# A float32 kernel of linear attention beside an MLP: three small moves of side work

## The chip, the cores and the metric

The kernel runs on one core of a Trainium2 chip. The metric is the time of one execution on the device, in microseconds (us). The kernel before took 713.92 us (median of three executions, 712.97 to 714.16).

## The reference

```python
x  = A_x                                     # 1 x 2048 tokens x 640
xn = layernorm(x)
# A: linear attention, 32 heads of 20, learned feature maps
q, k, v = split_heads(xn @ wqkv)
phi(u) = concat(softmax(u @ w_phi), softmax(-(u @ w_phi)))
o = phi(q) @ (phi(k).T @ v) / (phi(q) @ sum(phi(k)) + 1e-6)
A = merge_heads(o) @ wo
# B: an MLP over a second layernorm, hidden width 1728, tanh gelu
B = gelu(layernorm(xn) @ w1 + b1) @ w2 + b2
return x + A + B
```

## The kernel before, in words

All products are done in float32 split into two parts: a high part (a copy in the short float32r format) and a low part (the value less its high part). A full product takes three matmuls, high x high, high x low and low x high (`mm3`, L62 to L64). So every operand needs a copy on ScalarE and a subtraction on VectorE or GpSimd before TensorE can use it.

The 2048 tokens are four blocks of 512. First the MLP is computed for blocks 0 and 1, then keys, values and queries are projected, then the MLP for blocks 2 and 3 runs with the attention beside it, then the output projection. This text is about the first of these stages, from 50 to 215 us.

The hidden width is cut into 14 chunks of 128, of which chunk 13 is half a chunk (64). Chunks go in pairs, group g being chunks 2g and 2g+1. For a group and a block, the first layer fills one PSUM bank a chunk, ScalarE applies gelu, and a high and a low part are made; the second layer (`second`) then runs for m = 0 to 4 through three PSUM banks in turn: six matmuls (five with the half chunk) into a bank, and then VectorE adds the bank to the accumulator (L313, L311 for group 0). So the bank of m can be filled again for the third m after it only once VectorE has added it up. For groups 2 to 5 a scheme with fewer products is used (`cycle`), whose second layers stand between the products of the next group.

Group 6 holds the half chunk. In `passes` its 64 rows of high weight and its 64 rows of low weight share one matmul, and so L288 to L292 follow: ScalarE copies half of the bank, VectorE adds the other half (L289), ScalarE applies gelu (L290) and makes the high part (L291), and L292 makes the low part, which only the second layer of that block reads. `self.tail` says which engine does L292: in this stage VectorE, in the later MLP stage GpSimd.

Beside the MLP runs a chain of side work, a generator called `side` (`prep`). TensorE's code advances it once after each three matmuls; one such advance is called a step here. `prep` first waits two steps; then VectorE subtracts a column from the feature-map weights (L681, into the tile `wpt`), and at the same step the first *folds* follow (L612: small matmuls of the key and query weights with `wpt`, into two further banks, which ScalarE and VectorE then copy out, L630 and L632). After the folds, ten chunks of x of blocks 2 and 3 are normalised: a load (L674), GpSimd subtracts the mean (L695), VectorE multiplies (L703), ScalarE makes the high part (L709), VectorE the low part (L712), and both are stored (L714). The last of the ten falls in group 6.

In group 6 a second chain, `last_weights`, loads the v weights (L821), makes their high parts on ScalarE and their low parts on GpSimd (L53 and L56 through `split`, tiles `wkh` and `wkl`), and copies the k weights in (L823).

ScalarE, VectorE and GpSimd do their work in the order in which this code issues it, each engine strictly in order; so an instruction that waits holds up all behind it. The loads and stores go through one queue (SP), whose order a scheduler of the framework decides when the program is built.

Of the kernel before, what the change touches and what calls it, by code (L numbers as in the profile page):

```python
# [11 lines left out]
ALU = mybir.AluOpType  # L12
# [26 lines left out]
def f(ap):  # L39
    return ap.bitcast(F32)  # L40
# [3 lines left out]
def tile_kernel(ctx: ExitStack, tc: tile.TileContext, x, xT, wkT, wqT, wv, wphi, wo, w1, b1, w2, b2,  # L44
                ident, mmask, emask, vsel, out):
    nc = tc.nc
    ctx.enter_context(nc.allow_low_precision(reason="float32 operands are split exactly into float32r parts"))

    def split(hi, lo, src, scale=None, eng=nc.vector, first=nc.scalar):

        if scale is None:
            if first is nc.scalar:
                nc.scalar.activation(hi, src, AF.Copy)  # L53
            else:
                first.tensor_copy(hi, src)
            eng.tensor_tensor(lo, src, f(hi), op=ALU.subtract)  # L56
        else:
            nc.scalar.activation(hi, src, AF.Copy, scale=scale)
            nc.vector.scalar_tensor_tensor(lo, src, scale, f(hi), op0=ALU.mult, op1=ALU.subtract)
# [37 lines left out]
    class Banks:  # L97

        def __init__(self, *ids):
            self.ids, self.n = ids, 0  # L100
# [11 lines left out]
    def mtile(i, dtype=F32):  # L112
        return mp.tile([P, 2, D if i < 5 else 512], dtype, name=f"m{i}")
# [87 lines left out]
    class Mlp:  # L201
        def __init__(self, slots, hid):
            self.hid, self.turn, self.slots, self.beside, self.raw, self.tiles, self.spare = hid, 0, slots, iter(()), {}, {}, nc.vector
            self.tail = nc.gpsimd
            self.ph, self.px, self.po = Banks(0, 1, 2), Banks(3, 4), Banks(5, 6, 7)
            self.hold, self.held = False, []

# [59 lines left out]
        def passes(self, g, b, ws, hid=None):  # L267


            yh, yl = y[b]  # L270
            self.turn ^= 1
            todo = ()
            if hid is None:
                hid, todo, gts = [], ws, mtile(4)
            for j, (w1h, w1l, w2h, w2l) in enumerate(todo):
                gt = gts[:, j, :512]
                hs = mtile(self.hid[self.turn][j], F32R)
                hh, hl = hs[:, 0, :512], hs[:, 1, :512]
                if not (g == 6 and j == 1):
                    self.first(g, j, b, ws[j], gt, hh, hl)  # L280
                    hid.append((hh, hl))
                else:
                    pz = self.ph()
                    for kc in range(KC):
                        nc.tensor.matmul(pz, w1h[:, kc, :], yh[:, kc, :], start=kc == 0, stop=False)  # L285
                        nc.tensor.matmul(pz, w1l[:, kc, :], yl[:, kc, :], start=False, stop=kc == KC - 1)  # L286
                    tm = gt[0:64, :]
                    nc.scalar.activation(tm, pz[64:128, :], AF.Copy)  # L288
                    nc.vector.tensor_tensor(tm, pz[0:64, :], tm, op=ALU.add)  # L289
                    nc.scalar.activation(gt[0:64, :], tm, AF.Gelu_apprx_tanh, bias=b1t[0:64, 13:14])  # L290
                    nc.scalar.activation(hh[0:64, :], gt[0:64, :], AF.Copy)  # L291
                    self.tail.tensor_tensor(hh[64:128, :], gt[0:64, :], f(hh[0:64, :]), op=ALU.subtract)  # L292
                    hid.append((hh, None))
            yield
            yield from self.second(g, b, hid, ws)
# [28 lines left out]
    mlp = Mlp((0, 1, 2, 3), ((0, 2), (1, 3)))  # L324

    def finish(p):
        for _ in p:
            pass
# [66 lines left out]
    raw = [mlp.raw[c] for c in range(2)]  # L395
# [106 lines left out]
    def hi(t, src, eng=None):  # L502
        return lambda: nc.scalar.activation(t[0], src, AF.Copy)

    def lo(t, src, eng):
        return lambda: eng.tensor_tensor(t[1], src, f(t[0]), op=ALU.subtract)
# [72 lines left out]
    def raws(n, g):  # L579
        raw = fp.tile([P, D], F32, name="raw")  # L580
        if g < 5:
            nc.sync.dma_start(raw, {"k": wkT, "q": wqT}[n][g * G6:g * G6 + P, :])
        else:
            nc.sync.dma_start(raw[:2 * DH], wkT[5 * G6:])
            nc.sync.dma_start(raw[2 * DH:], wqT[D - P + 2 * DH:])
        return raw
# [64 lines left out]
    def ahead(loads, n):  # L651

        todo, ready = iter(loads), []
        for _ in loads:
            while len(ready) <= n:
                load = next(todo, None)
                if load is None:
                    break
                ready.append(load())
            yield ready.pop(0)  # L660
# [10 lines left out]
    def prep():  # L671
        def load(b, c):
            xc = fp.tile([P, D], F32, name="raw")[:, :512]
            nc.sync.dma_start(xc, xT[c * P:(c + 1) * P, b * 512:(b + 1) * 512])  # L674
            return xc

        todo = [(b, c) for b in range(2, 4) for c in range(KC)]
        loads = ahead([*(lambda job=job: raws(*job) for job in jobs), *(lambda job=job: load(*job) for job in todo)], 1)
        for _ in range(2):
            yield  # L680
        nc.vector.tensor_tensor(wpt[:, :, :, 1:], wpt[:, :, :, 1:], wpt[:, :, :, 0:1].to_broadcast([P, 6, 6, DF]), op=ALU.subtract)  # L681
        more = chain(more_stats(), rows(fp, mlp.px))
        for i, _ in enumerate(folds(loads)):
            if i % 10 in (5, 7, 9):
                next(more, None)
            yield
        fs.close()
        finish(more)
        mrs = [row_pair(b, fp.tile([P, 2, 512], F32, name="t", bufs=2).rearrange("p a c -> p (a c)")) for b in range(2, 4)]
        for _ in range(6):  # L690
            yield

        def centred(b, c):
            xc = next(loads)
            nc.gpsimd.tensor_tensor(xc, xc, mrs[b - 2][:, 0], op=ALU.subtract)  # L695
            return xc

        following = centred(*todo[0])
        for _ in range(4):
            yield  # L700
        for i, (b, c) in enumerate(todo):
            xc = following
            nc.vector.tensor_tensor(xc, xc, mrs[b - 2][:, 1], op=ALU.mult)  # L703
            yield
            if i + 1 < len(todo):
                following = centred(*todo[i + 1])
            yield
            hi = fp.tile([P, D], F32R, name="xs", bufs=3)[:, :512]
            nc.scalar.activation(hi, xc, AF.Copy)  # L709
            for _ in range(2):  # L710
                yield
            nc.vector.tensor_tensor(xc.bitcast(F32R), xc, f(hi), op=ALU.subtract)  # L712
            for p, src in enumerate((f(hi), xc)):
                nc.sync.dma_start(y_dram[b - 2][p][:, c, :], src)  # L714
            for _ in range(4):
                yield
# [9 lines left out]
    def cycle(g, other, side):  # L726
# [3 lines left out]
        bank, v, a = {}, nc.vector, nc.scalar  # L730
# [35 lines left out]
        if g < 5:  # L766
            events += weight_events({"11": 3, "S1": 4, "S3": 5, "s1": 7, "s2": 10, "S4": 11, "D5": 12, "12": 15, "15": 16, "s3": 18,
                                       "22": 22, "25": 23, "s4": 27, "d5": 28}, g + 2)
        else:
            def take(c):  # L770
                def go():
                    mlp.raw[c] = araw[c - 12], r2[c - 12]
                    ready[c] = mlp.take_parts(c, mlp.tiles[c % 4])
                    ready[c][1][0]()
                return go

            mlp.spare, mlp.tail = nc.gpsimd, nc.vector
            events += [(16, take(12)), (19, take(13))]
        mlp.beside = both(at_steps(*((when - 1, what) for when, what in events)), side)
        bank["a"] = mlp.ph()  # L780
# [27 lines left out]
    for g in range(2, 6):  # L808
        before = cycle(g, before, side)
# [3 lines left out]
    wkv_ = [kvw.tile([P, KC, CB[2]], F32R, name=f"wk{p}") for p in "hl"]  # L813

    def last_weights():

        events = []
        for kc in range(KC):
            k, v = slice(0, F1), slice(F1 + 2 * F2, CB[2])
            raw = f(wkv_[1][:, kc, v])  # L820
            events += [(2 * kc, lambda kc=kc, raw=raw: nc.sync.dma_start(raw, wv_dram[:, kc])),  # L821
                       (2 * kc + 7, lambda kc=kc, raw=raw: split(wkv_[0][:, kc, v], wkv_[1][:, kc, v], raw, eng=nc.gpsimd)),
                       *((2 * kc + 10 + p, lambda kc=kc, p=p: nc.sync.dma_start(f(wkv_[p][:, kc, k]), wk_dram[p][:, kc])) for p in range(2))]  # L823
        return at_steps(*events)

# [36 lines left out]
    for i in range(2):  # L862
        v = vp.tile([P, 11 * VS], F32R, name=f"v{i}")
# [121 lines left out]
    for t, i in [(t, i) for t in range(13) for i in range(4)] + [(13, 0), (13, 1), (13, 2), (14, 0), (14, 1), (13, 3), (14, 2), (15, 0), (15, 1),  # L985
# [30 lines left out]
        if i == 0 and t in (1, 2, 3, 6, 7):  # L1016

            kc = (1, 2, 3, 6, 7).index(t)
# [7 lines left out]
        if (t, i) == (11, 0):  # L1026
            mlp = Mlp((0, 2, 3, 1), ((1, 2), (0, 3)))
# [305 lines left out]
    for g in range(7):  # L1333
        for b in range(2, 4):
# [24 lines left out]
            if (g, b) == (0, 3):  # L1359
# [5 lines left out]
                op = ctx.enter_context(tc.tile_pool(name="oB", bufs=1, reuse_waits="tile"))  # L1365
# [189 lines left out]
```

## Time and profile before

| | |
|---|---|
| median of the runs | 713.92 us (712.97 to 714.16) |
| profiled execution, whole | 713.56 us |
| its span, first to last instruction | 711.8 us |
| TensorE busy | 701.5 us, 99% |
| VectorE, GpSimd, ScalarE busy | 507.6, 439.4, 352.9 us |

Times of the trace count from the first instruction. PE is TensorE, DVE VectorE, ACT ScalarE, POOL GpSimd, SP the queue that issues transfers. Matmuls are pipelined: one may start 0.23 us after the one before it although its row shows 0.39 us, so it is the starts that tell the pace.

### The profile page before, as it was taken

Reading aid. Unit: us, or ns where it says so; the run is one execution under the profiler, and the core shown is the slowest. Engines: PE = TensorE matmul, PEld = TensorE weight load, DVE = VectorE, ACT = ScalarE, POOL = GpSimd, SP = SyncE. Lnnn points to the kernel's source line nnn. Section 1 sums busy time; section 2 is a strip of 40 time slices with the busy share of each in tenths; the row PEclk is TensorE's granted clock in tenths of the full one; section 3 lists DMA queues with packets and bytes.
Section 4 is the critical chain, followed back from the end, with each engine's and each line's share of the span. In section 5 each row is a group of like instructions: output and inputs, shape, how many; then the busy total and the mean of one; then the engine's idle time right before and its main releaser. Section 6 shows DMA issues by size and latency. Waiting matters only on the chain.

```text
span 711.8 us, 9916 instructions
## 1 busy us (share of the span) xinstructions
PE 701.5 (99%) x3368; PEld 592.2 (83%) x3368; DVE 507.6 (71%) x839; ACT 352.9 (50%) x624; POOL 439.4 (62%) x408
## 2 busy tenths in 40 slices
PE   8999999999899999999999999999999999999998
PEld 7888888888678888888888888888888888888886
DVE  7877875588554798898878887755575656778653
ACT  7844646445513564464355448455565556551310
POOL 2586434676442897797787878656587777553400
PEclk9999999999999999999999999999999999999999
DMA  9615966557651223723600705674444653163222
GB/s 328 267 41 196 297 176 195 136 183 236 260 231 83 93 75 148 182 93 151 148 1 1 186 0 189 165 212 128 134 129 120 206 157 105 46 234 120 90 75 88
DMA packets 77894, 105.05 MB, mean 148 GB/s; under 512 B 22884, under 2 KB 46068, under 8 KB 76220
## 3 DMA queue, kind: packets, MB, share of 16 engines
q1 hardware_dynamic: 77844, 104.43, 46.6%
q8 instruction: 26, 0.43, 0.3%
q14 instruction: 24, 0.20, 0.1%
HBM read 71.43 MB, written 34.61 MB: 149 GB/s over the span
## 4 chain that ended last, share of the span: by engine, by line
PE 90%; DMA 4%; DVE 2%; ACT 1%; POOL 1%; issue 1%; SPq 1%; ACTq 0%
PE bank L62 27%; PE bank L63 27%; PE bank L64 27%; PE bank L946 3%; DMA r<-in_w 2%; DMA wv__79<-in_wv 2%; PE bank L612 2%; PE bank L1175 1%; PE bank L1174 1%; PE bank L308 1%; PE bank L309 1%; DMA raw<-in_wkT 1%; PE bank L286 0%; PE bank L285 0%; DVE acc L311 0%
## 5 line engine op out<-in xcount | busy, mean ns | idle before, releaser
L62 PE MATMUL bank<-m,w 128*128 128x512 f32 x266 | 105.8, 398 | 4.0 <-DVE acc L313 3.7
L62 PE MATMUL bank<-y,w 128*128 128x512 f32 (+1 forms) x270 | 104.6, 387 | 0.0
L64 PE MATMUL bank<-m,w 128*128 128x512 f32 x266 | 104.3, 392 | 0.0
L64 PE MATMUL bank<-y,w 128*128 128x512 f32 (+1 forms) x270 | 104.3, 386 | 0.0
L63 PE MATMUL bank<-y,w 128*128 128x512 f32 (+1 forms) x270 | 104.2, 386 | 0.0
L63 PE MATMUL bank<-m,w 128*128 128x512 f32 x262 | 102.7, 392 | 0.0
L313 DVE TENSOR_TENSOR acc<-bank,acc 128x512 f32<-128x512 f32 x120 | 80.6, 681 | 23.3 <-PE bank L64 18.9
L62 PE MATMUL bank<-wkh,y 128*128 128x512 f32 (+2 forms) x240 | 87.6, 365 | 0.0
L63 PE MATMUL bank<-wkl,y 128*128 128x512 f32 (+2 forms) x240 | 87.1, 363 | 0.0
L64 PE MATMUL bank<-wkh,y 128*128 128x512 f32 (+2 forms) x240 | 86.9, 362 | 0.0
L911 POOL TENSOR_TENSOR m<-m,mx 128x640 f32<-128x640 f32 (+2 forms) x48 | 44.4, 937 | 47.8 <-DVE mx L899 47.8
L892 ACT ACTIVATE m<-bank 128x512 f32<-128x512 f32 (+1 forms) x64 | 26.5, 440 | 87.2 <-PE bank L64 66.6
L1168 POOL TENSOR_TENSOR e<-e,m 128x512 fp32r<-128x512 f32 (+1 forms) x28 | 39.5, 1412 | 39.1 <-ACT m L1167 34.9
L62 PEld LDWEIGHTS bank<-m,w 128*128 128x128 f32 x266 | 50.4, 189 | 15.7 <-DVE acc L313 5.0
L64 PEld LDWEIGHTS bank<-m,w 128*128 128x128 f32 x266 | 50.4, 189 | 10.7
L64 PEld LDWEIGHTS bank<-y,w 128*128 128x128 f32 x270 | 50.7, 188 | 10.3
L63 PEld LDWEIGHTS bank<-y,w 128*128 128x128 f32 x270 | 50.7, 188 | 10.1
L62 PEld LDWEIGHTS bank<-y,w 128*128 128x128 f32 x270 | 50.7, 188 | 10.1
L56 POOL TENSOR_TENSOR w<-r,w 128x640 fp32r<-128x640 f32 x31 | 48.5, 1584 | 16.6 <-ACT w L53 16.6
L918 DVE TENSOR_REDUCE sm<-m 128x64 f32<-128x1280 f32 x32 | 47.3, 1479 | 15.8 <-ACT m L916 15.6
L63 PEld LDWEIGHTS bank<-m,w 128*128 128x128 f32 x262 | 49.5, 189 | 9.7
L916 ACT ACTIVATE m<-m,rs_all 128x1280 f32<-128x1280 f32 x32 | 43.7, 1367 | 21.7 <-POOL m L911 21.4
(261 smaller groups left out, 1642.7 us busy)
## 6 DMA issues: line engine op xcount, KB each, us to landing
r<-in_w SPq DMA_DIRECT2D x43, 320.0 KB
e<-e SPq DMA_DIRECT2D x40, 256.0 KB
e<-acc SPq DMA_DIRECT2D x52, 160.0 KB
acc<-in_xT SPq DMA_DIRECT2D x4, 1280.0 KB
a<-in_w SPq DMA_DIRECT2D x9, 320.0 KB
xb<-in_x SPq DMA_DIRECT2D x8, 320.0 KB
xs<-in_x SPq DMA_DIRECT2D x8, 320.0 KB
raw<-in_xT SPq DMA_DIRECT2D x10, 256.0 KB
```

Source lines behind the costliest of these rows:

```text
L56: eng.tensor_tensor(lo, src, f(hi), op=ALU.subtract)
L62: nc.tensor.matmul(ps, lh, rh, start=first, stop=False, **kw)
L63: nc.tensor.matmul(ps, lh, rl, start=False, stop=False, **kw)
L64: nc.tensor.matmul(ps, ll, rh, start=False, stop=last, **kw)
L313: nc.vector.tensor_tensor(acc[b][:, m, :], pw, acc[b][:, m, :], op=ALU.add)
L612: nc.tensor.matmul(ps[:, c + i * kd:c + (i + 1) * kd], raw[n, g][:, (kc + i) * P:(kc + i + 1) * P], wpt[:, g, :kd // DF, 1:], start=True, ...
L892: return nc.scalar.activation(p3[:, :, c], ps.rearrange("p (h f) -> p h f", h=H), AF.Copy).ins
L911: subs[n, t] = nc.gpsimd.tensor_tensor(ep[:, s], a, b, op=ALU.subtract)
L916: exps[n, t] = nc.scalar.activation(e, e, AF.Exp, scale=rs_all[:, t:t + 1])
L918: nc.vector.tensor_reduce(sm, e.rearrange("p s (h f) -> p (s h) f", f=DH), axis=AX, op=ALU.add)
L946: nc.tensor.matmul(kvp[g // 2][:P, (g % 2) * 240:(g % 2) * 240 + 240].rearrange("p (s f) -> p s f", s=4), v[:, g * VS:g * VS + P], ft[:, : ...
L1168: nc.gpsimd.tensor_tensor(pl, e, f(ph), op=ALU.subtract)
```

## The change

Three edits. The low part L292 is done by GpSimd in both MLP stages, and the choice (`tail`) goes. `prep` waits four steps, not two, before L681 and the first fold, so that everything in `side` comes two steps later. The low parts of the v weights are made by VectorE, a step and a half after the copies of the high parts, and no longer by GpSimd. `hi` and `lo` are helpers that the kernel had (L502 and L505): `hi` issues the copy on ScalarE, `lo` the subtraction on the engine named.

```diff
--- before.py
+++ after.py
@@ -201,7 +201,6 @@
     class Mlp:
         def __init__(self, slots, hid):
             self.hid, self.turn, self.slots, self.beside, self.raw, self.tiles, self.spare = hid, 0, slots, iter(()), {}, {}, nc.vector
-            self.tail = nc.gpsimd
             self.ph, self.px, self.po = Banks(0, 1, 2), Banks(3, 4), Banks(5, 6, 7)
             self.hold, self.held = False, []
 
@@ -289,7 +288,7 @@
                     nc.vector.tensor_tensor(tm, pz[0:64, :], tm, op=ALU.add)
                     nc.scalar.activation(gt[0:64, :], tm, AF.Gelu_apprx_tanh, bias=b1t[0:64, 13:14])
                     nc.scalar.activation(hh[0:64, :], gt[0:64, :], AF.Copy)
-                    self.tail.tensor_tensor(hh[64:128, :], gt[0:64, :], f(hh[0:64, :]), op=ALU.subtract)
+                    nc.gpsimd.tensor_tensor(hh[64:128, :], gt[0:64, :], f(hh[0:64, :]), op=ALU.subtract)
                     hid.append((hh, None))
             yield
             yield from self.second(g, b, hid, ws)
@@ -676,7 +675,7 @@
 
         todo = [(b, c) for b in range(2, 4) for c in range(KC)]
         loads = ahead([*(lambda job=job: raws(*job) for job in jobs), *(lambda job=job: load(*job) for job in todo)], 1)
-        for _ in range(2):
+        for _ in range(4):
             yield
         nc.vector.tensor_tensor(wpt[:, :, :, 1:], wpt[:, :, :, 1:], wpt[:, :, :, 0:1].to_broadcast([P, 6, 6, DF]), op=ALU.subtract)
         more = chain(more_stats(), rows(fp, mlp.px))
@@ -774,7 +773,7 @@
                     ready[c][1][0]()
                 return go
 
-            mlp.spare, mlp.tail = nc.gpsimd, nc.vector
+            mlp.spare = nc.gpsimd
             events += [(16, take(12)), (19, take(13))]
         mlp.beside = both(at_steps(*((when - 1, what) for when, what in events)), side)
         bank["a"] = mlp.ph()
@@ -819,7 +818,8 @@
             k, v = slice(0, F1), slice(F1 + 2 * F2, CB[2])
             raw = f(wkv_[1][:, kc, v])
             events += [(2 * kc, lambda kc=kc, raw=raw: nc.sync.dma_start(raw, wv_dram[:, kc])),
-                       (2 * kc + 7, lambda kc=kc, raw=raw: split(wkv_[0][:, kc, v], wkv_[1][:, kc, v], raw, eng=nc.gpsimd)),
+                       (2 * kc + 7, hi([wkv_[0][:, kc, v]], raw)),
+                       (2 * kc + 8.5, lo([wkv_[0][:, kc, v], wkv_[1][:, kc, v]], raw, nc.vector)),
                        *((2 * kc + 10 + p, lambda kc=kc, p=p: nc.sync.dma_start(f(wkv_[p][:, kc, k]), wk_dram[p][:, kc])) for p in range(2))]
         return at_steps(*events)
```

In the changed kernel L205 to L820 have numbers lower by one. Bank and tile numbers are given anew in each build.

At the first fold, on VectorE: the last two additions of group 0's second layer for block 1 (L311), the addition of `bank_800`, which is m = 0 of group 1's (L313), the subtraction into `wpt`, and the first fold's copies. Before:

```order
L311 SCALAR_TENSOR_TENSOR acc_103<-bank_768,b2t,acc_103 128x512
L311 SCALAR_TENSOR_TENSOR acc_103<-bank_780,b2t,acc_103 128x512
L681 TENSOR_TENSOR wpt<-wpt 128x36x19
L632 TENSOR_TENSOR t<-bank_807,t 128x384
L632 TENSOR_TENSOR restl<-bank_807,resth 128x4x18
L313 TENSOR_TENSOR acc_103<-bank_800,acc_103 128x512
```

and changed:

```order
L310 SCALAR_TENSOR_TENSOR acc_103<-bank_768,b2t,acc_103 128x512
L310 SCALAR_TENSOR_TENSOR acc_103<-bank_780,b2t,acc_103 128x512
L312 TENSOR_TENSOR acc_103<-bank_800,acc_103 128x512
L680 TENSOR_TENSOR wpt<-wpt 128x36x19
L631 TENSOR_TENSOR t<-bank_822,t 128x384
L631 TENSOR_TENSOR restl<-bank_822,resth 128x4x18
```

The subtraction into `wpt` now stands behind the addition of `bank_800`, not ahead of it.

At the same place on TensorE, where m = 0 of group 1's second layer for block 1 fills `bank_800`. Before:

```order
L63 MATMUL bank_800<-m_685,w_191 128x512
L64 MATMUL bank_800<-m_685,w_191 128x512
L612 MATMUL bank_807<-wpt,raw 128x114 x4
L612 MATMUL bank_808<-wpt,raw 128x114 x4
L62 MATMUL bank_800<-m_710,w_192 128x512
L63 MATMUL bank_800<-m_710,w_192 128x512
L64 MATMUL bank_800<-m_710,w_192 128x512
L62 MATMUL bank_835<-th_124,w_190 128x512
```

and changed:

```order
L63 MATMUL bank_800<-m_685,w_191 128x512
L64 MATMUL bank_800<-m_685,w_191 128x512
L62 MATMUL bank_800<-m_710,w_192 128x512
L63 MATMUL bank_800<-m_710,w_192 128x512
L64 MATMUL bank_800<-m_710,w_192 128x512
L62 MATMUL bank_813<-th_124,w_190 128x512
L63 MATMUL bank_813<-tl_128,w_190 128x512
L64 MATMUL bank_813<-th_124,w_190 128x512
L611 MATMUL bank_822<-wpt,raw 128x114 x4
L611 MATMUL bank_823<-wpt,raw 128x114 x4
```

The fold's matmuls, which read `wpt`, moved behind the second half of `bank_800` and three more matmuls: six matmuls later.

In group 6, on VectorE, from the last chunk's multiplication on; `bank_1955` and `bank_1957` are the half chunk's banks, and the `acc_103` rows are m = 0 to 4 of group 5's second layer. Before:

```order
L703 TENSOR_TENSOR raw<-raw,t 128x512
L56 TENSOR_TENSOR m_1930<-m_1929,m_1930 128x512
L289 TENSOR_TENSOR m_1929<-bank_1957,m_1929 64x512
L292 TENSOR_TENSOR m_1956<-m_1929,m_1956 64x512
L712 TENSOR_TENSOR raw<-raw,xs 128x512
L313 TENSOR_TENSOR acc_103<-bank_1978,acc_103 128x512
L313 TENSOR_TENSOR acc_103<-bank_1990,acc_103 128x512
L313 TENSOR_TENSOR acc_103<-bank_2001,acc_103 128x512
L313 TENSOR_TENSOR acc_103<-bank_2012,acc_103 128x512
L313 TENSOR_TENSOR acc_103<-bank_2024,acc_103 128x512
```

and changed:

```order
L702 TENSOR_TENSOR raw<-raw,t 128x512
L56 TENSOR_TENSOR m_1927<-m_1926,m_1927 128x512
L288 TENSOR_TENSOR m_1926<-bank_1955,m_1926 64x512
L312 TENSOR_TENSOR acc_103<-bank_1976,acc_103 128x512
L711 TENSOR_TENSOR raw<-raw,xs 128x512
L312 TENSOR_TENSOR acc_103<-bank_1987,acc_103 128x512
L505 TENSOR_TENSOR wkl<-wkl,wkh 128x640
L312 TENSOR_TENSOR acc_103<-bank_2000,acc_103 128x512
L505 TENSOR_TENSOR wkl<-wkl,wkh 128x640
L312 TENSOR_TENSOR acc_103<-bank_2011,acc_103 128x512
L505 TENSOR_TENSOR wkl<-wkl,wkh 128x640
L312 TENSOR_TENSOR acc_103<-bank_2023,acc_103 128x512
```

L292 is gone from VectorE, the addition of m = 0 stands ahead of the last chunk's low part (`raw<-raw,xs`), and the v weights' low parts stand between the additions.

At the same place on ScalarE. Before:

```order
L709 ACTIVATE xs<-raw 128x512 x2
L260 ACTIVATE m_1929<-bank_1931,b1t 128x512
L53 ACTIVATE m_1930<-m_1929 128x512
L288 ACTIVATE m_1929<-bank_1957 64x512
L290 ACTIVATE m_1929<-m_1929,b1t 64x512
L291 ACTIVATE m_1956<-m_1929 64x512
L53 ACTIVATE w_189<-r_1735 128x640
L244 ACTIVATE w_190<-r_1783 128x640
L53 ACTIVATE wkh<-wkl 128x640 x4
```

and changed:

```order
L287 ACTIVATE m_1926<-bank_1955 64x512
L289 ACTIVATE m_1926<-m_1926,b1t 64x512
L290 ACTIVATE m_1954<-m_1926 64x512
L53 ACTIVATE w_189<-r_1733 128x640
L243 ACTIVATE w_190<-r_1780 128x640
L708 ACTIVATE xs<-raw 128x512
L502 ACTIVATE wkh<-wkl 128x640 x4
L837 ACTIVATE wkh<-resth 128x5x192
```

The last chunk's high part (`xs<-raw`) moved from ahead of the half chunk's work to behind the copies of the second-layer weights.

On SP, the last load of a chunk of x (`raw<-in_xT`). Before:

```order
L714 DMA yl_76<-raw 128x512
L821 DMA wkl<-wv__79 128x640 x3
L674 DMA raw<-in_xT 128x512
L821 DMA wkl<-wv__79 128x640
L714 DMA yh_75<-xs 128x512
L821 DMA wkl<-wv__79 128x640
L823 DMA wkh<-wkh 128x512
L823 DMA wkl<-wkl 128x512
```

and changed:

```order
L820 DMA wkl<-wv__79 128x640
L823 DMA wkh<-wkh 128x512
L823 DMA wkl<-wkl 128x512
L823 DMA wkh<-wkh 128x512
L823 DMA wkl<-wkl 128x512
L713 DMA yh_75<-xs 128x512
L823 DMA wkh<-wkh 128x512
L823 DMA wkl<-wkl 128x512
L673 DMA raw<-in_xT 128x512
L713 DMA yl_76<-raw 128x512
```

That load moved behind six of the ten copies of the k weights.

## Rows read from the trace of the kernel before

**Rows 1.** The page, part 1: busy us (share of the span) xinstructions

```profile
PE 701.5 (99%) x3368; PEld 592.2 (83%) x3368; DVE 507.6 (71%) x839; ACT 352.9 (50%) x624; POOL 439.4 (62%) x408
```

**Rows 2.** Waits of PE: engine line <- what ended it: us, times, longest

```profile
PE bank L62 <- DVE acc L313: 3.7, 2, 2.1
```

**Rows 3.** Timeline of PE, 188 to 207: start, us, engine, line, op, out<-in, [idle<-releaser]

```profile
188.87 0.39 PE L63 MATMUL bank<-m,w 128*128 128x512 f32 x1
189.10 0.39 PE L64 MATMUL bank<-m,w 128*128 128x512 f32 x1
191.63 0.60 PE L62 MATMUL bank<-m,w 128*128 128x512 f32 x1 [2.15 <-DVE acc L313]
...
204.92 0.39 PE L309 MATMUL bank<-m,w 128*128 128x512 f32 x1
206.84 0.50 PE L62 MATMUL bank<-m,w 128*128 128x512 f32 x1 [1.53 <-DVE acc L313]
```

**Rows 4.** Stretches: PE busy (x) PEld, DVE, ACT, POOL, PEclk, DMA, GB/s

```profile
191.90:195.30 3.40, 3.40 (x9) 2.62 (x9) 1.57 (x3) 2.45 (x4) 3.40 (x3) 0.50 0.20 74
...
205.30:207.00 1.70, 0.17 (x2) 0.16 (x2) 1.59 (x3) 0.05 (x1) 0.00 (x0) 1.00 0.00 0
```

**Rows 5.** Timeline of DVE, 186 to 191

```profile
186.07 0.68 DVE L289 TENSOR_TENSOR m<-bank,m 64x512 f32<-64x512 f32 x1 [0.76 <-ACT m L288]
188.21 0.69 DVE L292 TENSOR_TENSOR m<-m,m 64x512 fp32r<-64x512 f32 x1 [1.45 <-ACT m L291]
188.93 2.05 DVE L712 TENSOR_TENSOR raw<-raw,xs 128x512 fp32r<-128x512 f32 x1
190.90 1.28 DVE L313 TENSOR_TENSOR acc<-bank,acc 128x512 f32<-128x512 f32 x2
```

**Rows 6.** Timeline of POOL, 188 to 202

```profile
188.88 1.55 POOL L56 TENSOR_TENSOR w<-r,w 128x640 fp32r<-128x640 f32 x1 [8.59 <-ACT w L53]
...
201.22 1.55 POOL L56 TENSOR_TENSOR wkl<-wkl,wkh 128x640 fp32r<-128x640 f32 x1
```

**Rows 7.** Timeline of DVE, 201 to 203

```profile
201.07 2.26 DVE L56 TENSOR_TENSOR m<-m,m 128x512 fp32r<-128x512 f32 x1 [4.10 <-ACT m L53]
```

**Rows 8.** Line L292 by engine: duration ns min/median/max, first and last start us, forms

```profile
L292 POOL TENSOR_TENSOR m<-m,m x2: 1292/1345/1398, 622.0 to 634.9; 64x512 fp32r<-64x512 f32 x2
```

**Rows 9.** Timeline of ACT, 187 to 189

```profile
187.54 0.63 ACT L291 ACTIVATE m<-m 64x512 fp32r<-64x512 f32 x1
...
188.71 0.72 ACT L244 ACTIVATE w<-r 128x640 fp32r<-128x640 f32 x1
```

**Rows 10.** Timeline of PE, 64 to 68

```profile
64.27 0.39 PE L64 MATMUL bank<-m,w 128*128 128x512 f32 x1
...
67.06 0.48 PE L62 MATMUL bank<-m,w 128*128 128x512 f32 x1
```

**Rows 11.** The chain in order of time: start us, us, what

```profile
74.14 1.77 PE bank L612 x16
```

**Rows 12.** Timeline of DVE, 63 to 65

```profile
63.73 0.85 DVE L681 TENSOR_TENSOR wpt<-wpt 128x684 f32<-128x684 f32 x1
```

**Rows 13.** Timeline of POOL, 65 to 67

```profile
65.31 1.54 POOL L506 TENSOR_TENSOR w<-r,w 128x640 fp32r<-128x640 f32 x1 [2.51 <-ACT w L503]
```

**Rows 14.** Timeline of ACT, 122 to 124

```profile
122.94 0.64 ACT L751 ACTIVATE m<-m 128x512 fp32r<-128x512 f32 x1
```

**Rows 15.** Timeline of DVE, 121 to 123

```profile
121.61 0.16 DVE L632 TENSOR_TENSOR restl<-bank,resth 128x12 fp32r<-128x12 f32 x1
...
122.28 0.16 DVE L632 TENSOR_TENSOR restl<-bank,resth 128x12 fp32r<-128x12 f32 x1
122.35 1.28 DVE L313 TENSOR_TENSOR acc<-bank,acc 128x512 f32<-128x512 f32 x2
```

**Rows 16.** Timeline of PE, 124 to 126

```profile
124.97 0.39 PE L62 MATMUL bank<-m,w 128*128 128x512 f32 x1
```

**Rows 17.** Timeline of POOL, 178 to 180

```profile
179.00 1.29 POOL L695 TENSOR_TENSOR raw<-raw,t 128x512 f32<-128x512 f32 x1 [5.27 <-DMA raw<-in_xT]
```

## The prediction

> **What bounds the kernel now.** The page's busy shares come first: TensorE is busy 99% of the span, VectorE 71%, GpSimd 62% [rows 1]. So only time in which TensorE stands still, or runs at its lower clock, can be won. The list of waits is read next: TensorE's longest sum is 3.7 us, two waits for VectorE's addition L313 [rows 2]. TensorE's timeline places them at 191.63 (2.15 us idle) and at 206.84 (1.53 us) [rows 3], both in group 6, where the change works. By the starts, which follow each other at 0.23 us (188.87, 189.10), the first matmul was due at 189.33 and came 2.30 late, the second due at 205.15 and came 1.69 late. The table of stretches adds a third loss: in the 3.40 us behind the first wait TensorE's clock was 0.50, the lower of its two levels (1.2 and 2.4 GHz); behind the second it stayed at 1.00 [rows 4]. Half speed for 3.40 us costs 1.70. These three, 5.7 us, are what can be won.
>
> VectorE's timeline says why. At the first wait its queue held L289, then L292, which could start only at 188.21 because it waits for ScalarE's L291, then L712, and only then the addition for m = 0, at 190.90 [rows 5]. L712 took 2.05, L292 of the same 512 columns 0.69: GpSimd's L56 started 0.05 before it and ran to 190.43, and L712 ended 0.55 behind that [rows 5, 6]. The second wait has the same form: VectorE's L56 took 2.26 beside a GpSimd L56 on a v weight that ended at 202.77 [rows 6, 7], so L289 and the chain behind it came late, with the additions queued behind L292.
>
> **The change part by part.** I count against the profiled execution's own 713.56 us (span 711.8 and 1.76 around it), which is 0.36 under the median of the runs.
>
> *L292 to GpSimd, second wait.* With L292 gone, VectorE goes from L289 straight to the additions. The GpSimd L56 that slowed VectorE is gone too (edit three), so L56 on VectorE takes about 0.7, and L289 waits only for ScalarE. The additions then start some 2.5 us before the bank is needed again. Gain 1.69. L292 itself takes 1.35 on GpSimd instead of 0.69 [rows 5, 8]; its reader is the second layer of the same block, at least one second layer later (25 matmuls, 5.7 us), and ahead of it on GpSimd stand only memsets, so it costs nothing; without that cover it would cost 0.7.
>
> *L292 to GpSimd and `side` two steps later, first wait.* The addition of m = 0 now follows L289, which ends at 186.75 [rows 5]; the bank is due at 189.33, so that wait goes. What is late next is m = 1. Ahead of its addition VectorE has L712, and L712's input, L709, has moved on ScalarE behind L291 and the two weight copies. L244 ends at 189.43 [rows 9]; L709 of the same 512 columns as L291 takes 0.63, so L712 can start at 190.06. By then GpSimd, which did L292 from 188.17 to 189.52, is in its L56 of 1.55 [rows 6], until 191.07. If L712 waits for it as it did before, it ends at 191.62; the addition starts 0.08 before that, and TensorE 0.73 after the addition's start, as at 190.90 and 191.63 [rows 3, 5]: at 192.27. Due is 189.33 + 6 x 0.23 = 190.71. The new wait is 1.56 in place of 2.30: gain 0.74. If L712 does not wait it ends at 190.75 and the loss shrinks to about 0.7: gain 1.6. I take the first, since L712's own row is the nearest.
>
> *The clock.* The new idle time is about 1.4 by the profile's count, nearer to the 1.53 that left the clock up than to the 2.15 that cost it [rows 3, 4]. I take the 1.70 as won; the other end is nothing won.
>
> *v low parts on VectorE.* Five subtractions leave GpSimd (1.55 each [rows 6]) and stand on VectorE between the additions of m = 1 to 4 and before the next L56. Those additions free banks that TensorE refills only from 199 on, behind the 25 matmuls of the next first layer, so even at 1.55 each they are covered. Cost nothing; if the cover were gone, up to 1.55 a piece.
>
> *`side` two steps later, first fold.* Before, TensorE was due to start the fold at 64.50 (0.23 after 64.27) and was through at 67.06 [rows 10]; sixteen such pieces take 1.77 [rows 11], so 0.79 was lost there. Now L681 stands behind the addition of `bank_800` on VectorE, whose last matmul starts at 64.96. That ends about 65.35, the addition takes 0.64 (two in 1.28 [rows 5]), so L681 starts near 66.0 instead of 63.73. Alone it takes 0.85 [rows 12]: 66.85. But GpSimd runs L506 from 65.31 to 66.85 [rows 13]; if L681 is held by it as L712 was by L56, it ends near 67.6. TensorE reaches the fold at 64.50 + 6 x 0.23 = 65.88 and starts 0.1 after L681: 66.95 to 67.7, a loss of 1.1 to 1.85. Against 0.79 the change costs 0.3 to 1.05 here. No row shows an L681 beside a GpSimd subtraction; the nearest row, L712's, was held by one, so I take 1.0.
>
> The Trainium skill bears on that choice (SBUF — State Buffer, "Who interferes with whom"): a VectorE instruction with two inputs in SBUF contends with a GpSimd instruction that reads SBUF, and the one that comes second is blocked for the whole of the other. By that rule L681 is held and the sum is the 710.9 above; without it, it is 710.2. L712's row agrees with the rule for that operation; for L681 no row here shows it.
>
> *`side` two steps later, elsewhere.* In group 3 the last fold's copies move on ScalarE behind L750 and L751, which ended at 123.58 [rows 14]. Two rounds between ScalarE's copies and VectorE's subtractions follow, 0.67 each (121.61 to 122.28 [rows 15]), and on VectorE the addition of m = 0 is queued behind them. It started at 122.99 (second of the pair of 122.35 [rows 15]); now it starts at 124.9, or 0.2 sooner since ScalarE has one round less ahead of L751, and frees its bank at 125.35. TensorE wants that bank at 124.97 [rows 16]. Cost 0.3 to 0.4, bounds 0 and 1; I take 0.3.
>
> Sum: -1.69 - 0.74 - 1.70 + 1.0 + 0.3 = -2.83. From 713.56 that is 710.7, from the median 711.1; I say 710.9.
>
> **The rivals.** *The clock falls once again.* There are two shorter waits now, 1.4 and up to 1.7 idle, against one of 2.15. For it: both are near 1.53 and nothing between 1.53 and 2.15 is shown. Against: at 1.53 it held. Price 1.70: 712.6.
>
> *The holds don't happen.* L712 and L681 find GpSimd free. Then 0.9 and 0.7 more are won: 709.3. Against it: L712 was held in the same place before.
>
> *The gain is nibbled away between 66 and 185.* Two steps move all the rows of the folds and of x on VectorE against the additions, and four waits of half a microsecond come up: 2 us lost, 712.9. For it: the tight place in group 3. Against: with as much side work before, TensorE's long waits lay elsewhere and it was busy 99% [rows 1, 2].
>
> *The last load comes late (slower).* On SP the last load of a chunk of x now stands behind six copies of k weights. Before, GpSimd's L695 stood 5.27 us waiting for it and started at 179.00 [rows 17]. L695 (1.29), L703 and L56 (0.6 each) must pass before L289 at 186.07; so nothing is lost until L695 starts at 183.6. From there each us of delay goes through L289, L291, L709 and L712 to TensorE, and at 0.6 us late the wait passes 2.15 idle and costs the clock 1.70. Slower than before by 0.2% it is from 186.2 on; at 187.5 the time is 711.1 + 3.9 + 1.7 = 716.7. Against: the later place in the queue would have to cost over 7 us.
>
> **How the numbers follow.** Within 0.2% (1.43 us), about what a measurement of this kernel can tell from no change, means 712.49 to 715.35. My forecast of 710.9 (its own range 709.9 to 711.9) gets 0.48; the clock 0.20; no holds 0.10; nibbled 0.12; the late load 0.10, six tenths of it past the point of slower. Faster: 0.48 + 0.10 + half of the clock's 0.20 and a little of the nibbling = 0.69. Slower 0.06. The rest, 0.25, is the same. The range runs from 709.0, where both holds are absent, to 713.6, which takes in one fall of the clock or the nibbling and leaves out the late load.
>
> **What would show it.** Right: no wait of TensorE in the second layer of group 6's block 0; one wait of 1.2 to 1.7 us at its last m before that, ended by L313 behind L711; a clock of 1.00 there; a wait of 1 to 1.7 us before the first L611, ended by VectorE's `wpt`. Wrong: a granted clock of 0.50 behind either wait; L694 starting after 183.6; new waits of TensorE for L312 between 70 and 185; or a VectorE row of the v weights' low parts in front of an addition that TensorE waits for.

## The result, and the profile after

The changed kernel is slower: 716.75 us, median of 11 executions (714.47 to 719.24), against 713.64 of the kernel before beside it (711.33 to 717.27, 11 executions); ratio 1.0043, 95% interval 1.0024 to 1.0061. Forecast was 710.9. The profiled execution took 716.18 with a span of 714.4, 2.6 more than before.

The page, part 1, and TensorE's waits from 60 to 240 us (they answer [rows 1, 2]):

```profile
PE 701.8 (98%) x3368; PEld 592.1 (83%) x3368; DVE 507.7 (71%) x842; ACT 353.0 (49%) x624; POOL 434.5 (61%) x405
```

```profile
PE bank L62 <- DVE acc L312: 4.7, 3, 3.3
PE bank L611 <- issue: 1.7, 1, 1.7
```

The busy shares hardly differ; the waits do. There were two waits for VectorE's addition, 3.7 us; there are three now, 4.7 us, and one of 1.7 ahead of the first fold. TensorE's timeline places the long ones (answers [rows 3]):

```profile
190.91 0.39 PE L64 MATMUL bank<-m,w 128*128 128x512 f32 x1
192.34 0.50 PE L62 MATMUL bank<-m,w 128*128 128x512 f32 x1 [1.04 <-DVE acc L312]
...
193.60 0.40 PE L64 MATMUL bank<-m,w 128*128 128x512 f32 x1
197.33 0.50 PE L62 MATMUL bank<-m,w 128*128 128x512 f32 x1 [3.33 <-DVE acc L312]
```

By the starts, 0.23 us apart, m = 0 came 1.20 late and m = 1 3.50 late. The wait at 206.84 us, in the second layer of group 6, is gone, as forecast. The stretches (busy us of PE, PEld, DVE, ACT, POOL, then PEclk; answer [rows 4]) show the clock at 0.50 for 3.4 us behind the waits, a loss of 1.7 as before, only later:

```profile
194.00:197.30 3.30, 0.00 (x0) 0.00 (x0) 2.39 (x3) 3.30 (x7) 3.09 (x4) 1.00 0.22 82
198.85:202.25 3.40, 3.40 (x10) 2.62 (x9) 3.40 (x6) 0.95 (x2) 2.66 (x4) 0.50 0.79 295
```

Who was late? SP's timeline, then GpSimd's, VectorE's and ScalarE's (answer [rows 17, 5, 6, 9]):

```profile
174.47 0.91 SPq L713 DMA_DIRECT2D yl<-raw  x1
175.42 0.65 SPq L820 DMA_DIRECT2D wkl<-wv__79  x1
176.50 0.32 SPq L823 DMA_DIRECT2D wkh<-wkh  x1
...
182.24 0.32 SPq L823 DMA_DIRECT2D wkl<-wkl  x1
183.02 0.33 SPq L673 DMA_DIRECT2D raw<-in_xT  x1
```

```profile
188.46 1.30 POOL L694 TENSOR_TENSOR raw<-raw,t 128x512 f32<-128x512 f32 x1 [10.59 <-DMA raw<-in_xT]
193.23 1.27 POOL L291 TENSOR_TENSOR m<-m,m 64x512 fp32r<-64x512 f32 x1 [3.47 <-ACT m L290]
194.58 1.54 POOL L56 TENSOR_TENSOR w<-r,w 128x640 fp32r<-128x640 f32 x1
```

```profile
189.80 0.69 DVE L702 TENSOR_TENSOR raw<-raw,t 128x512 f32<-128x512 f32 x1 [6.57 <-POOL raw L694]
190.41 0.68 DVE L56 TENSOR_TENSOR m<-m,m 128x512 fp32r<-128x512 f32 x1
191.01 0.68 DVE L288 TENSOR_TENSOR m<-bank,m 64x512 f32<-64x512 f32 x1
191.61 0.67 DVE L312 TENSOR_TENSOR acc<-bank,acc 128x512 f32<-128x512 f32 x1
194.91 1.77 DVE L711 TENSOR_TENSOR raw<-raw,xs 128x512 fp32r<-128x512 f32 x1 [2.62 <-ACT xs L708]
196.60 0.68 DVE L312 TENSOR_TENSOR acc<-bank,acc 128x512 f32<-128x512 f32 x1
```

```profile
187.26 0.60 ACT L287 ACTIVATE m<-bank 64x512 f32<-64x512 f32 x1 [0.85 <-PE bank L285]
191.72 0.72 ACT L289 ACTIVATE m<-m,b1t 64x512 f32<-64x512 f32 x1 [3.87 <-DVE m L288]
...
194.26 0.61 ACT L708 ACTIVATE xs<-raw 128x512 fp32r<-128x512 f32 x1
```

The last load of x is issued at 183.02, where it was 172.52 before. GpSimd stands 10.59 us for it, VectorE 6.57 behind GpSimd, and L288, whose input ScalarE had ready at 187.86 (L287, 187.26 + 0.60), starts at 191.01. The additions of m = 0 and m = 1 follow. L711 is late once more: its input stands on ScalarE behind the whole chain of the half chunk, and GpSimd's L56 holds it for 1.77 us.

Last, the first fold (TensorE, VectorE and GpSimd; answer [rows 10, 12, 13]):

```profile
65.59 0.39 PE L64 MATMUL bank<-th,w 128*128 128x512 f32 x1
67.65 1.56 PE L611 MATMUL bank<-wpt,raw 128*128 128x114 f32 x12 [1.68 <-issue]
```

```profile
65.94 1.61 DVE L680 TENSOR_TENSOR wpt<-wpt 128x684 f32<-128x684 f32 x1
```

```profile
65.28 1.55 POOL L505 TENSOR_TENSOR w<-r,w 128x640 fp32r<-128x640 f32 x1 [2.51 <-ACT w L502]
```

L680 took 1.61 where it had taken 0.85, and ended 0.72 behind GpSimd's L505: it was held, as the sum had assumed, and TensorE began the fold at 67.65 (bounds 66.95 to 67.7). The view puts this wait down to "issue" and not to VectorE's `wpt`, the sign that the prediction had named; that it was for `wpt` is shown below, in the run that moves only that subtraction.

The losses added up: before 0.79 at the fold, 0.07 at 152 us, 2.30 and 1.69 for the two waits, 1.71 for the clock, 6.56 in all. After: 1.83, 0.21 (at 125 us), 0.47 (at 152 us), 1.20, 3.50 and 1.71, 8.92. The difference, 2.36, is nearly all of the span's 2.6.

### The profile page after: what moved, and what is told of

It is laid out like the page before. It is cut to its first block, busy times and chain, and to the rows that moved or that the text cites. A ratio compares the mean times of both kernels' runs of the same rounds, so it can differ in the third digit from the quotient of the medians.

```text
span 714.4 us, 9919 instructions
## 1 busy us (share of the span) xinstructions
PE 701.8 (98%) x3368; PEld 592.1 (83%) x3368; DVE 507.7 (71%) x842; ACT 353.0 (49%) x624; POOL 434.5 (61%) x405
## 4 chain that ended last, share of the span: by engine, by line
PE 85%; DVE 5%; issue 3%; DMA 3%; ACT 2%; POOL 2%; POOLq 0%; ACTq 0%; SPq 0%; DVEq 0%
PE bank L62 25%; PE bank L63 25%; PE bank L64 25%; PE bank L946 3%; PE bank L611 2%; PE bank L1175 1%; PE bank L1174 1%; DMA raw<-in_xT 1%; DMA wkl<-wv__79 1%; DVE st L130 1%; PE bank L307 1%; PE bank L308 1%; DVE m L754 1%; DVE raw L711 1%; DVE raw L702 1%
## 5 line engine op out<-in xcount | busy, mean ns | idle before, releaser
L62 PE MATMUL bank<-m,w 128*128 128x512 f32 x266 | 105.5, 397 | 5.0 <-DVE acc L312 4.7
L62 PE MATMUL bank<-y,w 128*128 128x512 f32 (+1 forms) x270 | 105.1, 389 | 0.0
L62 PE MATMUL bank<-wkh,y 128*128 128x512 f32 (+2 forms) x240 | 87.6, 365 | 0.0
L62 PEld LDWEIGHTS bank<-m,w 128*128 128x128 f32 x266 | 50.0, 188 | 17.3 <-DVE acc L312 6.8
L62 PEld LDWEIGHTS bank<-y,w 128*128 128x128 f32 x270 | 51.0, 189 | 10.4
L64 PEld LDWEIGHTS bank<-m,w 128*128 128x128 f32 x266 | 49.9, 188 | 10.5
L56 POOL TENSOR_TENSOR w<-r,w 128x640 fp32r<-128x640 f32 x31 | 48.5, 1583 | 7.8 <-ACT w L53 7.6
```

The costliest lines, as they stand in the source:

```text
L62: nc.tensor.matmul(ps, lh, rh, start=first, stop=False, **kw)
L64: nc.tensor.matmul(ps, ll, rh, start=False, stop=last, **kw)
```

## The experiments

Theory A: the late load of the last chunk of x, which comes with the two added steps, is what cost the time, through the copies of k weights that stand ahead of it on SP. Rivals: edit one or edit three costs by itself (B); the two steps make x late whatever stands on SP (C), in the form that the load's tile comes free late (D); or they cost through the order on VectorE and ScalarE, load or no load (E).

Results; "stage" is the time between two TensorE starts in the profiled execution (the L62 that waits near 33.6 us in every kernel, and the last matmul of group 6's second layers), which leaves out what differs before and behind it. "Clock up" counts the executions whose mean granted clock was 0.999 or 1.000; for the kernel before they are those of the three later comparisons.

| kernel | median us | ratio to before (95%) | stage us | clock up |
|---|---|---|---|---|
| before | 711.51 to 713.64 in four comparisons | 1 | 181.18 | 39 of 69 |
| after (all edits) | 716.75 | 1.0043 (1.0024 to 1.0061) | 183.73 | 2 of 11 |
| edit 1 | 709.84 | 0.9963 (0.9949 to 0.9978) | 176.65 | 6 of 6 |
| edit 2 | 716.49 | 1.0060 (1.0045 to 1.0074) | 182.92 | 0 of 6 |
| edit 3 | 712.65 | 1.0002 (0.9986 to 1.0017) | 180.61 | 5 of 12 |
| edits 1, 3 | 707.78 | 0.9937 (0.9923 to 0.9951) | 175.30 | 6 of 6 |
| after, k copies on ScalarE's queue | 711.78 | 0.9995 (0.9982 to 1.0007) | 179.04 | 10 of 12 |
| after, own tile for the last chunk | 712.08 | 1.0004 (0.9989 to 1.0018) | 179.64 | 12 of 12 |
| after, `wpt` after two steps | 713.83 | 1.0022 (1.0006 to 1.0037) | 183.19 | 3 of 12 |
| after, own tile and `wpt` | 709.99 | 0.9969 (0.9955 to 0.9982) | 177.40 | 12 of 12 |
| edits 1, 3, and the load late | 716.17 | 1.0059 (1.0042 to 1.0076) | 183.76 | 0 of 6 |
| edits 1, 3, and one step | 710.92 | 0.9984 (0.9972 to 0.9996) | 178.03 | 12 of 12 |

**Edit one alone** (the hunks on `tail` of the diff above).

> Edit one alone: the half chunk's low part on GpSimd, everything else as before. Theory A (the late load of x, which comes with the two steps, is what cost the time): the load of the last chunk of x keeps its place on SP (about 172.5 us), VectorE goes from the half chunk's sum (ends 186.75) straight to L711 and the addition of m = 0, both ahead of GpSimd's L291 at 188.17, so TensorE waits neither at 189.3 nor at 205.2 and its clock stays up: 5.7 us of the profiled execution before (2.30 + 1.69 + 1.70) go, some 708 us. Theory B (the low part on GpSimd itself costs, since its 1.35 us push GpSimd's subtractions of the weights back into VectorE's way): TensorE still stands more than 2 us in group 6, its clock falls, 712 us or more.

Both waits and the fall of the clock went, and 4.53 us of the stage with them, so B falls for edit one. But 1.36 us came back in a place neither theory named; TensorE's waits from 60 to 240 us, and GpSimd's timeline:

```profile
PE bank L307 <- POOL m L291: 1.4, 1, 1.4
```

```profile
199.64 2.48 POOL L863 MEMSET v<- 128x1408 f32 x2
202.09 1.57 POOL L56 TENSOR_TENSOR wkl<-wkl,wkh 128x640 fp32r<-128x640 f32 x1
203.74 1.26 POOL L291 TENSOR_TENSOR m<-m,m 64x512 fp32r<-64x512 f32 x1
```

In block 1 the input of L291 was ready at 200.28 (ScalarE's L290) and TensorE wanted its result at 203.53, but on GpSimd L291 is queued behind the low parts of the v weights and the memsets, and it ended at 205.00.

**Edit two alone** (`range(2)` becomes `range(4)` in `prep`).

> Edit two alone: prep begins two steps later, the half chunk's low part stays on VectorE and the v weights' low parts on GpSimd. Theory A (late load): L674's last transfer is issued near 183 us and lands near 188; L292 stands ahead of the addition of m = 0 on VectorE, starts near 193.2, and TensorE stands 3.3 us there and runs 3.4 us at 0.50 behind it; the wait in the second layer of group 6 stays (1.7), and the first fold starts 1.8 late: losses of 1.83 + 0.2 + 0.5 + 3.5 + 1.7 + 1.7 = 9.4 in place of 6.6, some 716.5 us. Theory B (edits one or three cost the time): 711 to 714 us, with the load landing before VectorE needs it.

716.49, with the waits at the places named (2.81 and 0.95 idle, both smaller than expected). Within the intervals it costs alone what the whole change costs.

**Edit three alone** (the two lines of `last_weights`).

> Edit three alone: the v weights' low parts on VectorE, a step and a half after their copies; the half chunk's low part stays on VectorE, prep begins after two steps. Theory A (edit three costs nothing and removes only the GpSimd subtraction that slowed VectorE's L56 at 201 us): the first wait of 2.15 us idle and the 3.4 us at 0.50 stay, VectorE's L56 takes 0.7 in place of 2.26, so the second wait shrinks from 1.53 to about 0.5; gain 1.0 to 1.2 us, some 712.4 in the profiled execution. Theory B (the low parts on VectorE hold up additions that TensorE waits for): new waits of TensorE for L313 between 192 and 200 us and a time of the kernel before or more.

The waits were 2.15 and 0.86 idle, none between them: A's reading, though the second was expected near 0.5. The 0.6 us that the stage won are too few to show in the medians, and this profiled execution (714.96) was the longest of its kernel.

**Edits one and three, without edit two.**

> Edits one and three without edit two: the change, but prep begins after two steps as before. Theory A (late load): as with edit one alone, no wait of TensorE over 0.8 us apart from the 0.8 at the first fold, clock 1.00 throughout group 6, some 708 us, 8 us under the changed kernel. Theory B (the v weights' low parts on VectorE, between the additions, are what delays them): TensorE waits 1 to 3 us for L312 near 195 to 200 us, and the time is 711 us or more.

All of TensorE's waits from 60 to 240 us, and its clock across both old places:

```profile
PE bank L611 <- DMA raw<-in_wkT: 0.3, 1, 0.3
```

```profile
186.00:194.00 8.00, 8.00 (x37) 6.63 (x36) 6.52 (x7) 7.23 (x11) 5.27 (x5) 1.00 0.61 223
200.00:208.00 8.00, 8.00 (x37) 6.64 (x36) 5.13 (x11) 0.64 (x1) 1.29 (x1) 1.00 0.42 174
```

5.88 us of the stage are gone, more than the 4.53 and 0.57 of its halves: edit three clears GpSimd for L291, so the two need each other. This version beats both kernels.

**The k copies on ScalarE's queue.**

```diff
-                       *((2 * kc + 10 + p, lambda kc=kc, p=p: nc.sync.dma_start(...
+                       *((2 * kc + 10 + p, lambda kc=kc, p=p: nc.scalar.dma_start(...
```

> The changed kernel, all three edits, but the ten copies of the k weights (L823) are issued on ScalarE's queue in place of SP's, so that on SP the last load of x stands directly behind two stores of x. Theory A (the load is late because of the copies ahead of it on SP): the load is issued near 176.5 us and GpSimd's L694 starts near 182; the first wait of group 6 is the one that was forecast (about 1.4 us idle, at m = 1) or none, the clock stays up; the losses at the first fold (1.83) and at 125 and 152 us (0.2 and 0.5) stay: some 711 us. Theory C (the two steps make x late by themselves, whatever stands on SP, because its buffer comes free later and the shift of 1.8 us pushes all back): the load is issued after 181 us again, TensorE stands over 2 us, 715 us or more.

The time is A's, the load is C's. SP's timeline and its waits from 174 to 184 us:

```profile
173.46 0.80 SPq L713 DMA_DIRECT2D yl<-raw  x1
174.30 0.67 SPq L820 DMA_DIRECT2D wkl<-wv__79  x1
176.53 0.32 SPq L713 DMA_DIRECT2D yh<-xs  x1
181.43 0.33 SPq L673 DMA_DIRECT2D raw<-in_xT  x1
```

```profile
SPq L673 <- DMA yl<-raw: 4.5, 1, 4.5
```

and of the kernel before (waits from 166 to 175 us):

```profile
170.45 0.32 SPq L714 DMA_DIRECT2D yl<-raw  x1
170.87 1.34 SPq L821 DMA_DIRECT2D wkl<-wv__79  x3
172.52 0.33 SPq L674 DMA_DIRECT2D raw<-in_xT  x1
```

```profile
SPq L674 <- DMA yl<-raw: 1.7, 2, 1.5
```

With SP empty the load is still issued at 181.43: it waits until the store `yl` of an earlier chunk has left the tile it is to fill. Before, that store was issued at 170.45, directly ahead of the five loads of v weights, and the load followed at 172.52; of the 1.7 us of SP's two waits only 0.2 are this load's, 1.5 are those of the load at 167.19. Two steps later the store stands behind four of these loads, each 320 KB, and ends 8 us after its issue. So of the 10.5 us between 172.52 and 183.02 the tile alone makes some 8.9 and the copies at most 1.6. The changed kernel's own trace divides it more closely. The semaphores of its stores and loads tell when each landed: the store issued at 174.47 had landed at 182.22, in before the one issued at 170.45 at 172.46. What held SP from 182.22 on was the fifth load of v weights, as the chain that ended last shows:

```profile
175.42 7.58 DMA wkl<-wv__79
183.01 0.02 issue
183.02 5.28 DMA raw<-in_xT
```

That makes 9.7 for the tile and 0.8 for the queue. Off SP the copies were issued from 189.54 on, and so they no longer shared the transfer with the load either: GpSimd's L694 starts at 185.01, 3.6 after the issue, where in the changed kernel it was 5.4. Even this late it does not move L288 at all (187.81, ready at 187.78), and the loss of 4.7 and the clock turns into the one forecast wait, 1.61 idle.

**A tile of its own for the last chunk.**

```diff
-            xc = fp.tile([P, D], F32, name="raw")[:, :512]
+            xc = own[0].tile([P, 512], F32, name="x9") if (b, c) == todo[-1] else fp.tile([P, D], F32, name="raw")[:, :512]
```

(`own[0]` is a pool opened where the folds' pool closes.)

> The changed kernel, all three edits, but the last chunk of x is loaded into a tile of its own, so that its load need not wait until a store has left one of the three tiles that the chunks take in turn; on SP it then stands ahead of the loads of the v weights, everything else keeps its place. Theory D (the load is late because its tile comes free late: the store of an earlier chunk is issued behind the loads of the v weights and ends only near 181): the load is issued near 171 us, GpSimd's L695 starts before 183.6, TensorE has one wait of about 1.6 us at m = 1 of group 5's second layer (VectorE's subtraction held by GpSimd's), its clock stays at 1.00: as with the k weights on ScalarE's queue, a span near 709.6, some 711.3 us. Theory E (the two steps cost the time through VectorE's and ScalarE's order, load or no load): the waits of 1.04 and 3.33 and the clock of 0.50 stay, 716 us.

The load left at 128.39, not near 171 as expected, and GpSimd began on it at 177.47; the copies stayed on SP, and the clock was up in all 12 executions: this is D. E falls as the main cause, but is what is left:

```profile
194.78 0.50 PE L62 MATMUL bank<-m,w 128*128 128x512 f32 x1 [1.60 <-DVE acc L312]
```

```profile
192.32 1.80 DVE L712 TENSOR_TENSOR x<-x,xs 128x512 fp32r<-128x512 f32 x1 [2.49 <-ACT xs L709]
194.04 0.68 DVE L312 TENSOR_TENSOR acc<-bank,acc 128x512 f32<-128x512 f32 x1
```

```profile
192.01 1.56 POOL L56 TENSOR_TENSOR w<-r,w 128x640 fp32r<-128x640 f32 x1
```

This is the forecast wait at m = 1, held low part and all. With it, and with the fold, the change without its late load is worth nothing in the medians.

**The subtraction into `wpt` after two steps, the folds after four.**

```diff
-        for _ in range(4):
+        for _ in range(2):
             yield
         nc.vector.tensor_tensor(wpt[:, :, :, 1:], ..., op=ALU.subtract)
+        for _ in range(2):
+            yield
```

> The changed kernel with the subtraction into wpt issued after two steps as before, the folds after four. On VectorE it stands ahead of the addition of bank_800 again, nothing else moves. If the fold's late start comes from that subtraction's place: it starts near 63.7 us, ends 0.85 later, TensorE starts the fold without the 1.68 us idle, and 1.5 to 1.8 us of the changed kernel go; the waits in group 6 (1.04 and 3.33 idle, clock 0.50 behind) stay as they are, so some 714.5 us. If the fold waits for something else that came with the two steps (its load, its banks), TensorE still stands there and the time is that of the changed kernel, 716.2.

The fold started without a wait. TensorE's timeline:

```profile
65.83 0.39 PE L64 MATMUL bank<-th,w 128*128 128x512 f32 x1
66.06 1.93 PE L611 MATMUL bank<-wpt,raw 128*128 128x114 f32 x16
```

So it was `wpt` that the fold had waited for. The median is 2.9 under that of the changed kernel, but before beside it was 1.7 faster too; by ratio 0.2% are left, and the two intervals overlap. (With the own tile, below, the same edit is worth 2.1 us, clear of noise.) The profiled execution, 716.87, hides the gain, since its clock was low for about twice as long, from 195.1 to 202.0, at nearly the same waits (1.09 and 3.33 idle):

```profile
196.00:202.20 6.20, 6.20 (x16) 4.79 (x17) 6.20 (x8) 2.23 (x3) 3.53 (x5) 0.52 0.69 259
```

**Both cures together** (the last two edits).

> Both cures together: the changed kernel with the last chunk's own tile and with the subtraction into wpt after two steps. If the two losses are independent they add: no wait at the first fold, one wait of about 1.6 us in group 6, a span near 707.8, some 709.5 us; that is still above the kernel without the two steps (span 705.9) by that wait and by the 0.6 at 125 and 152 us. If one hides the other: 711 us or more.

They add: 709.99, no wait at the fold, one of 1.60 in group 6. It stays 2.1 us of the stage above edits one and three: edit two has a price beyond the load, mostly that wait.

**A late load without the two steps**: edits one and three, and the condition of the own tile is `(b, c) in (todo[-3], todo[-1])`, so that two chunks share it.

> Edits one and three, prep after two steps (no step added), but the chunks of x two before the last and the last share one tile, so that the last load must wait for a store of that tile and stands on SP behind nine of the ten copies of the k weights. Apart from the tile nothing of the two steps is in it. Theory A/D (a late load of the last chunk is enough to cost the time): load issued near 184 us, landing near 188.5, GpSimd's subtraction then, and VectorE's and ScalarE's chain behind it (ScalarE's copy of the chunk stands ahead of the gelu here), so the addition of m = 0 starts near 194.7 and TensorE stands some 6 us there and runs 3.4 us or more at 0.50: 7.8 us over the same kernel without it, some 715.5 us. Theory E (the load is covered, the steps cost by VectorE's order): 708 to 709 us.

GpSimd's timeline, TensorE's wait, and its clock behind it:

```profile
188.57 1.28 POOL L695 TENSOR_TENSOR x<-x,t 128x512 f32<-128x512 f32 x1 [14.88 <-DMA x<-in_xT]
```

```profile
195.06 0.80 PE L62 MATMUL bank<-m,w 128*128 128x512 f32 x1 [5.61 <-DVE acc L312]
```

```profile
194.60:201.30 6.70, 6.24 (x16) 4.99 (x17) 5.17 (x6) 6.70 (x10) 5.45 (x5) 0.55 0.22 71
```

The best version becomes as slow as the changed one by the load alone, issued at 183.20. A late load is enough.

**One step in place of two** (edits one and three, `wpt` after two steps, then one `yield` ahead of the folds).

> Edits one and three, the subtraction into wpt after two steps, folds and x one step later in place of two. On SP the last load of x then stands behind the loads of the v weights and one copy of the k weights; on VectorE the last chunk's low part stands behind the addition of m = 0, as in the changed kernel. Theory A/D: the load is issued near 177 us and lands in time (GpSimd's subtraction starts before 183.6), so the late load costs nothing; what is left of edit two is the wait of 1.6 us at m = 1 where GpSimd's L56 holds VectorE's low part: 1.8 us over the kernel without a step, less 0.3 at the first fold, some 709.3 us. If the load is late with one step too: TensorE stands over 2 us in group 6, its clock falls, 712 us or more.

The load was issued at 175.02 and GpSimd began at 181.20, in time; the wait at m = 1 is there (1.60 idle). Two waits that I had not forecast, 0.51 and 0.24 idle near 149.8 and 153.1 us, make the rest of the 2.7 us over the kernel without a step.

## Why the prediction was wrong, point by point

*L292 to GpSimd, second wait: right.* It went, worth 1.69. "So it costs nothing" held only because edit three takes the five subtractions off GpSimd; without that the cover is gone and TensorE waits 1.36.

*First wait: the mechanism right, hidden by the load.* Where the load was in time the wait at m = 1 was 1.60 idle, 1.75 late, against a forecast 1.56; L712 was held for 1.80 by GpSimd's L56, as taken.

*The clock: half right.* Waits of 1.36 to 1.61 idle left it up in 52 of 54 executions of five kernels. But I counted 1.70 as paid each time before; among the 69 executions of before beside the experiments the mean clock was under 0.999 in 30, with a median of 713.4 against 711.3 for the other 39. The profiled execution was one of the dear ones, so an estimate of this term over all executions is 0.9 (30/69 of 2.1). So this term was mis-sized too, and that is part of why, even with the load in time, the change took as long as before beside it (ratios 0.9995 and 1.0004) and not 2.8 us less.

*v low parts on VectorE: right.* No wait for them in any run.

*First fold: right*, 1.04 in place of 1.0, by the hold that was assumed: L680 ended 0.72 behind GpSimd's L505. The rule of the Trainium skill that was weighed there (SBUF — State Buffer, "Who interferes with whom"), one of the two blocked for the whole of the other, agrees with that row and with L712's 1.80 against 0.67 with edit one alone, where no GpSimd instruction ran beside it. *Group 3: right*, 0.21 for 0.3; 0.40 more at 152 us was a small case of the rival that nibbles.

*The step that failed* is the last rival's "the later place in the queue would have to cost over 7 us", which gave it one chance in ten and put it at nothing in the sum. It cost 10.5. I priced the place among SP's issues, six copies, and that was indeed worth at most 1.6 (0.8 in the changed kernel's trace). What the load waits for before it may be issued was not asked: its tile, which a store must leave, and edit two moves that store too, from ahead of the v weights to behind four of their five loads. The rival's price, one us for each us behind the limit and 1.70 for the clock, is near what was measured, but its limit was early: TensorE came to m = 0 1.8 us later than before (due at 191.14, not 189.33), so that by estimate 183.6 becomes 185.4, and a start at 185.01 did cost nothing. A start at 188.46 then makes 3.1 + 1.7 = 4.8 us; 4.69 of the stage lie between the changed kernel and the one with the k copies on ScalarE's queue. By the limit of 183.6 it would have been 717.7, against a median of 716.75. Without that one load, the sum from the runs is -1.69 - 0.55 - 1.70 + 1.04 + 0.21 + 0.40 = -2.3 against the profiled execution, near the forecast -2.83 and near the 2.14 by which the stage was shorter with the k copies on ScalarE's queue.

## What to carry to other kernels

When side work is moved, follow each load back to what must leave its tile, and ask where that store now stands among the other transfers; the load's own place in the queue is the smaller half. A short fixed delay is safe only as long as every chain it shifts has slack at its last link, which is the last chunk here. And of two edits that share an engine, the one may be what keeps the other free: price them together.

## What the runs showed of the hardware

The same program does not always pay for the same wait. Behind the 2.15 us of idle TensorE the clock was at 0.50 for 3.4 us in the profiled execution of before, yet 39 of 69 executions kept a mean of 0.999 or more, and those took 711.3 in the median, not 713.4. With a wait of 3.33 us idle it was low for 3.4 us in the changed kernel's profiled execution, from 1.5 us after TensorE was busy again, and for about 6.8 in another kernel with nearly the same waits, from 0.7 us before. Over the 11 executions of the changed kernel the mean was 0.999 or more in two, 0.998 in five and 0.995 in four; the two took 714.47 and 714.70, still some 3 us more than before with its clock up, so the clock alone does not make the change slow. With 5.61 us idle all six executions had a mean of 0.995. What decides this from one execution to the next no run here shows.
